# Batch 0's maximum of k, spread over the partitions by fp32 matmuls with an identity, and a new order of steps and loads

## The chip, the cores and the metric

The kernel runs on one core of a Trainium2 chip. The metric is the device time of one execution in microseconds (us). Before the change it is 240.76 us, the median of three runs (240.58 to 240.86). Engines are named as the profile names them: PE (TensorE, matmuls) and PEld (its weight loads), DVE (VectorE), ACT (ScalarE), POOL (GpSimd), SP (SyncE, which here only issues DMAs).

## What is computed

A linear attention over 8 batches, 8 heads, 576 positions and 64 channels, followed by a feed-forward block on 4608 tokens of 512 channels. All inputs and the output are fp32.

```python
q_s = exp(q - max(q, axis=-1));  q_s /= sum(q_s, axis=-1) + 1e-9
k_s = exp(k - max(k, axis=2));   k_s /= sum(k_s, axis=2) + 1e-9     # axis 2: the positions
kv  = einsum('bhsd,bhse->bhde', k_s, v)
x   = einsum('bhsd,bhde->bhse', q_s, kv)          # heads side by side: 4608 x 512
out = (((x @ w1) * (x @ w2)) @ w3) @ w_out        # 512 -> 1024 -> 1024 -> 512
```

The change is about `max(k, axis=2)` of batch 0: a maximum over positions, which lie on partitions as well as along the free dimension.

## The kernel before

**Steps and their order.** The kernel is written as named steps, such as `kmx.0.0` or `up.1.3.0.2`. Each step has an engine, the steps it needs, and the ring of PSUM or SBUF buffers from which it takes one. A long list written into the file, `ORDER`, gives the order in which the steps are emitted, and so the order of each engine's queue; `PICKS` says which engine does a step that has a choice (copies, subtractions, products). Each engine takes its own queue strictly in order and waits where a step's input isn't there. `FILL` puts in matmuls of zeros at the start. For the first `LINKED` steps of the list, steps of DVE and POOL marked as using the shared port are also chained to each other in list order.

**Folding the weights.** As `w3` and `w_out` are applied one after the other, the kernel first makes their product W3O. For each block ft of 128 rows of `w3` (0 to 7): `w3t.ft` transposes the block with eight fp16 matmuls against an identity (L439), `w3T.ft` copies it from PSUM (L322), `pf.ft.0` and `pf.ft.1` multiply it with the two halves of `w_out` (four matmuls of 512 columns each, L451), and `W3O.ft` scales it into place (L326 on ACT, L328 on DVE). The loads are `w3.3`, `w3.4` (blocks 4 and 5), `w3.1`, `w3.0`, `w3.5` (blocks 6 and 7), `w3.2` and `wo.0`, `wo.1`.

**Attention, per batch b.** A tile has the 576 positions of a head as 64 partitions times 9 along the free dimension; partitions 0 to 63 hold heads 0 to 3, partitions 64 to 127 heads 4 to 7.
- k: `kmx` takes the maximum over the 9 (a tree of four tensor_tensor for batches 0 to 3, L492 to L495), which leaves `km`, 128 x 256. `cb` takes it over the 64 partitions of each half and spreads it back: a transpose of 32x32 blocks (L499), a maximum (L502), four small instructions that swap neighbouring groups of 32 partitions (L505), one that joins them (L508), and a transpose back (L510). `ksub` subtracts it from k (two halves, L514), `kexp` is the exponential on ACT (L522), `kv` the product with v and the sums (L539, L549), `kv2` the division by the sums (L558 to L561).
- q: `qmx`, `qsub`, `qexp`, `qsm`, `qeps`, `qrc`, `qn` make the softmax over channels, in two parts (j 0 to 3 is part 0, j 4 to 8 part 1). For batches 0 and 1 `qt` transposes it on PE in groups of eight or two blocks (`qt.0.8`, `qt.0.16`, `qt.0.0`, L620) and `qT` copies it out; later batches use a DMA transpose (`qd`).
- `xm` and `xt` multiply q with kv2 (L653), `xs` and `xts` copy the result into x.

**Feed-forward, per chunk c of 512 tokens.** `up.1` and `up.0` multiply x with w2 and w1 (L767), `bs` copies the first result out of PSUM, `ab` takes the product (DVE, L782), `down` multiplies with W3O (L789, L804), `os` copies it out and `st` stores it. A ninth chunk takes the ninth j of every batch.

**Loads.** The first two loads (q of batch 0) are issued by SP, the list `LOADS` by POOL, one after the other, later ones (`LATE`) by SP. The POOL issue of load number i waits until load number i - 8 has landed: `w1.0` waits for `k.0`, `w1.1` for the load behind `k.0`, and `w2.1` for the one behind that. `k.1` waits for `wo.1`. A POOL issue also stands in POOL's queue behind the computing steps that come before it in the list.

**PSUM.** Three rings: "pab" with four buffers (`w3t`, `up`), "po" with two (`pf`, `down`), "att" with two (`kv`, `qt`, `xm` of the early batches).

**The list around the change** runs, on PE: w3t.3, w3t.4, w3t.5, pf.3.0, pf.4.0, pf.3.1, qt.0.8, pf.4.1, w3t.1, qt.0.16, pf.5.0, pf.5.1, qt.0.0, w3t.0, pf.1, pf.0.0, w3t.7, pf.0.1, w3t.2, pf.7.0, w3t.6, pf.7.1, pf.2.0, kv.0, pf.2.1, xm.0.0, pf.6, xm.0.1, and then the first `up`. (A step named without its half means both halves.)

Of the kernel before, what the change touches and what calls it, by code (L numbers as in the profile page):

```python
# [10 lines left out]
F32 = mybir.dt.float32  # L11
# [6 lines left out]
class Plan:  # L18
# [56 lines left out]
LINKED = 559  # L75

ORDER = """
q.0.1 qmx.0.1 q.0.0 qsub.0.1 qmx.0.0 qexp.0.1 w3.3 w3.4 wo.0 wo.1 w3.1 ident qsub.0.0 w3t.3 w3T.3
k.0 w3.0 w3t.4 qsm.0.1 qexp.0.0 qeps.0.1 qrc.0.1 w3T.4 w3t.5 pf.3.0 pf.4.0 qsm.0.0 qeps.0.0 pf.3.1
W3O.3 w3.5 w3.2 q.1.0 qn.0.1 qt.0.8 pf.4.1 w3t.1 qrc.0.0 w3T.5 v.0 k.1 w2.0 qn.0.0 qt.0.16 pf.5.0  # L80
w3T.1 W3O.4 qT.0.8 pf.5.1 kmx.0.0 cb.0 qt.0.0 w3t.0 W3O.5 ksub.0.1 w3T.0 pf.1.0 pf.1.1 pf.0.0 W3O.1
ksub.0.0 w3t.7 pf.0.1 w3T.7 qT.0.0 qT.0.16 kexp.0.1 W3O.0 w3t.2 pf.7.0 w3t.6 w3T.2 qmx.1.0 kexp.0.0
pf.7.1 w1.0 W3O.7 qsub.1.0 pf.2.0 w1.1 w2.1 k.2 w3T.6 kv.0 kv2.0 pf.2.1 qexp.1.0 xm.0.0 qsm.1.0
xs.0.0.1 pf.6.0 pf.6.1 xs.0.0.0 qeps.1.0 xm.0.1 xs.0.1.0 up.1.0.0.0 xs.0.1.1 up.0.0.0.0 up.1.0.1.0
w2.2 kmx.1.0 qrc.1.0 w1.2 cb.1 w2.3 w1.3 v.1 qn.1.0 bs.0.0.0 up.0.0.1.0 up.1.0.0.1 ab.0.0.0 W3O.2
qt.1.0 ksub.1.0 q.1.1 up.0.0.0.1 bs.0.1.0 up.1.0.1.1 bs.0.0.1 ab.0.1.0 qT.1.0 xt.0 ab.0.0.1 bs.0.1.1
kmx.2.0 up.0.0.1.1 up.1.0.0.2 ab.0.1.1 up.0.0.0.2 up.1.0.1.2 up.0.0.1.2 xts.0.0 xts.0.1 kexp.1.0
bs.0.0.2 ab.0.0.2 up.1.0.0.3 up.0.0.0.3 bs.0.1.2 up.1.0.1.3 ksub.1.1 cb.2 q.2 kexp.1.1 ab.0.1.2
up.0.0.1.3 v.2 W3O.6 bs.0.0.3 ab.0.0.3 kv.1 down.0.0 ksub.2.0 bs.0.1.3 kexp.2.0 kv2.1 ksub.2.1
xm.1.0 os.0.0 xs.1.0.1 xs.1.0.0 qmx.1.1 ab.0.1.3 kexp.2.1 down.0.1 qmx.2.0 qsub.1.1 up.1.1.0.0  # L90
up.0.1.0.0 up.1.1.0.1 up.0.1.0.1 qsub.2.0 vc.2.0 down.0.2 qmx.2.1 bs.1.0.0 qexp.1.1 os.0.1 vc.2.1
qexp.2.0 ab.1.0.0 qsm.1.1 bs.1.0.1 qeps.1.1 qsm.2.0 qsub.2.1 os.0.2 qrc.1.1 qn.1.1 ab.1.0.1 qeps.2.0
kv.2 up.1.1.0.2 up.0.1.0.2 up.1.1.0.3 kv2.2 qrc.2.0 up.0.1.0.3 qt.1.16 qt.1.8 down.0.3 qexp.2.1
qsm.2.1 bs.1.0.3 bs.1.0.2 qn.2.0 qeps.2.1 ab.1.0.3 ab.1.0.2 qrc.2.1 st.0.0 k.3 q.3 v.3 st.0.2 qT.1.8
qd.2.0 qn.2.1 st.0.1 qd.2.1 k.4 qT.1.16 xm.1.1 xs.1.1.0 xs.1.1.1 down.1.0 xt.1 qmx.3.1 up.1.1.1.0
qmx.3.0 kmx.3.0 up.0.1.1.0 up.1.1.1.1 os.0.3 up.0.1.1.1 bs.1.1.0 bs.1.1.1 cb.3 qsub.3.0 down.1.1
xts.1.1 xts.1.0 os.1.0 qexp.3.0 xm.2.0 ab.1.1.1 qsub.3.1 ab.1.1.0 xs.2.0.1 xs.2.0.0 up.1.1.1.2
up.0.1.1.2 qsm.3.0 xm.2.1 qexp.3.1 xs.2.1.0 xs.2.1.1 bs.1.1.2 ab.1.1.2 qsm.3.1 up.1.1.1.3 up.0.1.1.3
bs.1.1.3 ab.1.1.3 up.1.2.0.0 up.0.2.0.0 up.1.2.0.1 qeps.3.1 vc.3.0 kmx.4.0 bs.2.0.0 up.0.2.0.1
ab.2.0.0 qeps.3.0 bs.2.0.1 qrc.3.0 ksub.3.1 ksub.3.0 kexp.3.0 q.4 kexp.3.1 up.1.2.0.2 up.0.2.0.2  # L100
up.1.2.0.3 vc.3.1 os.1.1 qrc.3.1 ab.2.0.1 kmx.4.1 qmx.4.1 kv.3 down.1.2 up.0.2.0.3 qn.3.0 kv2.3 xt.2
bs.2.0.3 bs.2.0.2 qmx.4.0 ab.2.0.2 os.1.2 st.0.3 v.4 q.5 qd.3.0 qn.3.1 up.1.2.0.4 down.1.3
up.0.2.0.4 qsub.4.1 qd.3.1 qexp.4.1 ab.2.0.3 xts.2.1 xts.2.0 os.1.3 xm.3.0 xm.3.1 xt.3 bs.2.0.4
qsm.4.1 ab.2.0.4 qeps.4.1 xts.3.0 xs.3.0.1 xts.3.1 xs.3.0.0 up.1.2.0.5 bs.2.0.5 xs.3.1.1 xs.3.1.0
qsub.4.0 vc.4.0 cb.4 ksub.4.1 up.0.2.0.5 up.1.2.0.6 up.0.2.0.6 qexp.4.0 ab.2.0.5 ksub.4.0 up.1.2.0.7
up.0.2.0.7 qrc.4.1 qmx.5.1 bs.2.0.6 ab.2.0.6 vc.4.1 k.5 st.1.1 up.1.3.0.0 up.0.3.0.0 st.1.3 qsm.4.0
st.1.2 st.1.0 v.5 bs.2.0.7 qmx.5.0 ab.2.0.7 up.1.3.0.1 kexp.4.1 qeps.4.0 kexp.4.0 bs.3.0.0 qrc.4.0
kmx.5.1 down.2.0 up.0.3.0.1 kv.4 kmx.5.0 qn.4.1 os.2.0 vc.5.1 bs.3.0.1 v.6 qd.4.1 qn.4.0 qsub.5.0
cb.5 down.2.1 os.2.1 down.2.2 down.2.3 os.2.2 ab.3.0.0 kv2.4 up.1.3.0.2 qd.4.0 xm.4.0 os.2.3 xm.4.1
xt.4 ab.3.0.1 bs.3.0.2 up.0.3.0.2 xts.4.1 xts.4.0 up.1.3.0.3 up.0.3.0.3 up.1.3.0.4 qexp.5.0 ab.3.0.2  # L110
qsm.5.0 xs.4.0.0 ksub.5.0 kexp.5.0 bs.3.0.3 up.0.3.0.4 up.1.3.0.5 ab.3.0.3 xs.4.1.1 up.0.3.0.5
ksub.5.1 vc.5.0 qsub.5.1 kexp.5.1 xs.4.0.1 bs.3.0.4 qeps.5.0 ab.3.0.4 qexp.5.1 xs.4.1.0 up.1.3.0.6
# [795 lines left out]
```

## Time and profile before

| | |
|---|---|
| median of three runs | 240.76 us |
| the profiled execution, its own time | 240.74 us |
| its span, first to last instruction | 239.0 us |
| DVE busy | 180.8 us (76%) |
| ACT busy | 116.4 us (49%) |
| POOL busy | 110.2 us (46%) |
| DMA: bytes moved, mean rate | 45.66 MB, 191 GB/s |
| cb of batch 0, from its first to its last instruction's end | 22.30 to about 24.6 us |
| first `up` | 35.0 us |

The numbers come from one profiled execution; times within it count from the span's start. A line of a view names the source line (L439), the engine, the operation, the tile written and the tiles read, the shape and how many. Matmuls overlap, and their ends are modelled: the view of the chain of waits counts eight matmuls from the start of the first to the start of what follows, the timeline to the modelled end of the last. Square brackets at the end of a timeline line give the idle time of that engine just before it and what ended it.

### The profile page before, as it was taken

The page shows a single profiled execution, that of the slowest core. Times are in us where ns is not written, and L with a number is a line of the kernel's source. Part 1 is how long each engine was busy: PE and PEld are TensorE (multiplying, and loading weights), DVE is VectorE, ACT ScalarE, POOL GpSimd, SP SyncE. Part 2 cuts the span into 40 slices and gives each one's busy share as a digit, 9 for nine tenths or more (in the row PEclk, how much of TensorE's full clock was granted, in tenths as well). Part 3 has the DMA queues.
Part 4 walks back from the last instruction along what each step waited for, and adds up shares of the span by engine and source line. Part 5 has one row for each costly group of instructions (what it writes and reads, how often), then busy time and mean ns, then how long its engine had stood idle before and what let it go on. Part 6 is the DMA issues. An engine that isn't in the chain of part 4 may idle for free.

```text
span 239.0 us, 4957 instructions
## 1 busy us (share of the span) xinstructions
PE 231.4 (97%) x1987; PEld 121.4 (51%) x1987; DVE 180.8 (76%) x312; ACT 116.4 (49%) x185; POOL 110.2 (46%) x73
## 2 busy tenths in 40 slices
PE   7997999999999999999999999999999999999994
PEld 2543558867756544444444444444444444444442
DVE  2987998999899999998989989868577544443320
ACT  1625764659748848856935736452153012113211
POOL 8344178449939894989364795001910000000000
PEclk9999999999999999999999999999999999999998
DMA  6999999998999999899999302300659123030143
GB/s 206 217 293 238 321 219 295 241 392 281 393 187 323 401 220 303 298 260 347 342 390 254 91 1 44 58 0 0 134 121 198 44 58 76 0 91 0 44 132 132
DMA packets 37894, 45.66 MB, mean 191 GB/s; under 512 B 15984, under 2 KB 22384, under 8 KB 37872
## 3 DMA queue, kind: packets, MB, share of 16 engines
q1 hardware_dynamic: 30080, 34.22, 50.1%
q0 software_dynamic: 7792, 11.14, 21.2%
q8 instruction: 15, 0.25, 0.4%
q14 instruction: 7, 0.06, 0.1%
HBM read 38.80 MB, written 9.44 MB: 202 GB/s over the span
## 4 chain that ended last, share of the span: by engine, by line
PE 89%; DMA 7%; POOL 2%; issue 0%; ACT 0%; ACTq 0%; POOLq 0%
PE pab L767 53%; PE po L789 23%; DMA w<-in_moe_w_dram 7%; PE po L451 4%; PE po L804 3%; PE pkv L539 2%; PE xm L653 2%; PE w3t L439 1%; POOL w L401 1%; PE po L653 0%; PE pkv L549 0%; PE qtp L620 0%; POOL wosb L401 0%; POOL k L401 0%; PE xt L653 0%
## 5 line engine op out<-in xcount | busy, mean ns | idle before, releaser
L767 PE MATMUL pab<-x,w2sb 128*128 128x512 f16 (+1 forms) x320 | 66.0, 337 | 0.0
L767 PE MATMUL pab<-x,w1sb 128*128 128x512 f16 (+1 forms) x320 | 65.9, 337 | 0.0
L782 DVE TENSOR_TENSOR ab<-pab,bsb 128x512 f16<-128x512 f32 x72 | 48.5, 679 | 22.2 <-PE pab L767 20.1
L789 PE MATMUL po<-W3O,ab 128*128 128x512 f16 x256 | 59.4, 379 | 0.0
L322 ACT CAST bsb<-pab 128x512 f16<-128x512 f32 x52 | 30.2, 587 | 45.4 <-PE pab L767 38.4
L767 PEld LDWEIGHTS <-w1sb 128*128 128x128 f16 x352 | 34.1, 98 | 27.3
L767 PEld LDWEIGHTS <-w2sb 128*128 128x128 f16 x352 | 33.5, 98 | 27.3 <-issue 0.7
L605 POOL TENSOR_TENSOR en<-eq,qr 128x1024 f16<-128x1024 f16 (+1 forms) x13 | 26.8, 2075 | 28.1 <-issue 19.3
L789 PEld LDWEIGHTS <-ab 128*128 128x128 f16 x256 | 24.6, 98 | 29.0 <-issue 0.4
L514 POOL TENSOR_TENSOR k<-k,cb 128x1152 f32<-128x1152 f32 x13 | 34.0, 2625 | 11.0 <-DVE k L514 3.8
L322 ACT COPY osb<-po 128x512 f32<-128x512 f32 (+1 forms) x25 | 14.4, 577 | 34.9 <-PE po L789 27.6
L573 POOL TENSOR_TENSOR q<-q,qm 128x1280 f32<-128x1280 f32 (+1 forms) x13 | 27.7, 2142 | 7.5 <-DVE qm L568 4.1
L568 DVE TENSOR_REDUCE qm<-q 128x20 f32<-128x1280 f32 (+1 forms) x16 | 21.2, 1337 | 3.6 <-DMA q<-in_q_dram 3.6
L522 ACT ACTIVATE ek<-k 128x1152 f16<-128x1152 f32 x16 | 18.5, 1170 | 10.6 <-POOL k L514 9.3
L581 ACT ACTIVATE eq<-q 128x1280 f16<-128x1280 f32 (+1 forms) x16 | 18.7, 1170 | 6.6 <-POOL q L573 3.9
L586 DVE TENSOR_REDUCE qr<-eq 128x20 f32<-128x1280 f16 (+1 forms) x16 | 21.4, 1340 | 0.6 <-ACT eq L581 0.5
L322 DVE COPY osb<-po 128x512 f32<-128x512 f32 (+1 forms) x12 | 8.0, 667 | 15.5 <-PE po L789 8.3
L483 DVE TENSOR_REDUCE km<-k 128x128 f32<-128x1152 f32 x8 | 17.2, 2161 | 0.0
L322 DVE CAST bsb<-pab 128x512 f16<-128x512 f32 x20 | 13.7, 686 | 3.9 <-PE pab L767 3.6
L451 PE MATMUL po<-wosb,w3T 128*128 128x512 f16 x64 | 15.5, 379 | 0.5 <-DMA wosb<-in_moe_w_out_dram 0.5
L326 ACT ACTIVATE x<-xm 128x512 f16<-128x512 f32 x21 | 11.9, 603 | 3.2 <-PE xm L653 3.2
L349 PE MATMUL po<-zero 128*128 128x512 f16 x31 | 9.2, 457 | 1.6 <-DVE zero L344 1.6
(70 smaller groups left out, 193.2 us busy)
## 6 DMA issues: line engine op xcount, KB each, us to landing
out_dram<-osb SPq DMA_DIRECT2D x66, 128.0 KB, 2.5
q<-in_q_dram SPq DMA_DIRECT2D x6, 1152.0 KB, 8.0
v<-in_v_dram SPq DMA_DIRECT2D x6, 1152.0 KB, 8.9
k<-in_k_dram SPq DMA_DIRECT2D x5, 1152.0 KB, 7.2
k<-in_k_dram POOLq DMA_DIRECT2D x3, 1152.0 KB, 14.5
v<-in_v_dram POOLq DMA_DIRECT2D x2, 576.0 KB, 14.8
w<-in_moe_w_dram POOLq DMA_DIRECT2D x4, 256.0 KB, 14.4
w<-in_moe_w_dram POOLq DMA_DIRECT2D x2, 512.0 KB, 12.9
```

What stands on the lines that cost most here:

```text
L322: return [(nc.scalar.copy if eng == "ACT" else engine[eng].tensor_copy)(out=out, in_=in_)]
L451: nc.tensor.matmul(st["pf", ft], lhsT=st["w3T", ft][:, gt, :], rhs=wosb[:, gt, :], start=(gt == 0), stop=(gt == N_FT - 1))
L514: return [engine[eng].tensor_tensor(out=kb[:, two(hp), :, :], in0=kb[:, two(hp), :, :], in1=st["cb", b][:, two(hp), None, :].broadcast_to( ...
L522: nc.scalar.activation(out=st["ek", b][:, hp, :, :].rearrange("p j (i d) -> p i j d", i=2), in_=kb[:, two(hp), :, :], func=AF.Exp)
L568: dve.tensor_reduce(out=st["qm", b][:, :, j], in_=qb[:, :, j, :], axis=AX.X, op=ALU.max)
L573: return [engine[eng].tensor_tensor(out=qb[:, :, j, :], in0=qb[:, :, j, :], in1=st["qm", b][:, :, j, None].broadcast_to([P, HH, n, D]), op ...
L581: nc.scalar.activation(out=st["eq", b, p], in_=qb[:, :, j, :], func=AF.Exp)
L586: dve.tensor_reduce(out=st["qr", b][:, :, slice(*PARTS[p])], in_=st["eq", b, p], axis=AX.X, op=ALU.add)
L605: return [engine[eng].tensor_tensor(out=st["en", b][:, j, :, :].rearrange("p j h d -> p h j d"), in0=st["eq", b, p], in1=st["qr", b][:, :, ...
L767: nc.tensor.matmul(st["p", one, c, sub, u][:, a * (t1 - t0):(a + 1) * (t1 - t0)], lhsT=w[:, ct, fb * P:(fb + 1) * P], rhs=x()[:, ct, t0:t1 ...
L782: dve.tensor_tensor(out=st["ab", c][:, nf * u:nf * u + nf, t0:t1], in0=cut(st["p", 0, c, sub, u]), in1=cut(st["bsb", c, sub, u]), op=ALU.mult)
L789: nc.tensor.matmul(st["po", c, tb], lhsT=st["ab", c][:, ft, tb * P:(tb + 1) * P], rhs=W3O[:, ft, :], start=(ft == 0), stop=(ft == N_FT - 1))
```

## The change

For batch 0 (`PEK = [0]`) the step `cb` is replaced by three:
- `kT`: km, as two halves of 128 columns, is transposed by two fp32 matmuls against an fp32 identity into PSUM.
- `kr`: DVE takes the maximum over each group of 64 of the transposed columns, 128 x 256 to 128 x 4.
- `kB`: four fp32 matmuls with the identity as the moving operand. Each takes one column of kr, repeated 64 times, as the weights, so that the maximum appears on 64 partitions. The result stays in PSUM, and `ksub`, now always on DVE for batch 0, reads it there.

`kT` and `kB` take a buffer of the ring "pab". A new step `ident32` copies the identity to fp32 on ACT. The other batches keep `cb`. The rest of the new code (`CBX`, `KVE`, `kc`) is for settings that are off.

`ORDER`, `PICKS` and `LATE` are written anew over the whole program, `LINKED` goes from 559 to 580, and in `LOADS` w3.5 and w3.0 change places.

```diff
-LINKED = 559
+LINKED = 580
...
 LOADS = [
-    ("w3", 3), ("w3", 4), ("wo", 0), ("wo", 1), ("w3", 1), ("k", 0), ("w3", 0), ("w3", 5),
+    ("w3", 3), ("w3", 4), ("wo", 0), ("wo", 1), ("w3", 1), ("k", 0), ("w3", 5), ("w3", 0),
...
+    plan.add(("ident32",), "ACT", 0.28, lambda: nc.scalar.copy(out=ident32, in_=ident16), needs=[("ident",)],
+             lead=200.0)
...
+        def kT():
+            st["kT", b] = kbank("kT")
+            for n in range(NHP):
+                nc.tensor.transpose(st["kT", b][:, n, :], st["km", b].rearrange("p h d -> p (h d)")[
+                    :, n * P:(n + 1) * P], ident32)
...
+        def kr():
+            st["kr", b] = work.tile([P, NHP, G], F32, tag="kr", name="kr")
+            dve.tensor_reduce(out=st["kr", b], in_=st["kT", b].rearrange("p n (g r) -> p n g r", g=G),
+                              axis=AX.X, op=ALU.max)
...
+        def kB():
+            st["kB", b] = kbank("kB")
+            for n in range(NHP):
+                for gg in range(G):
+                    nc.tensor.matmul(st["kB", b][gg * HALF:(gg + 1) * HALF, n, :],
+                                     lhsT=st["kr", b][:, n, gg:gg + 1].broadcast_to([P, HALF]),
+                                     rhs=ident32, start=True, stop=True)
+            if not b:
+                st["cb", b] = st["kB", b].rearrange("p n (i d) -> p (n i) d", d=D)
...
-        A(("cb", b), "DVE", 2.25, cb, kms)
+        if b in PEK:
+            A(("kT", b), "PE", 0.45, kT, kms + [("ident32",)], takes=kring)
+            A(("kr", b), "DVE", 0.45, kr, [("kT", b)], gives=[("kT", b)])
+            A(("kB", b), "PE", 0.45, kB, [("kr", b)], takes=kring)
```

The new list on PE around this place: w3t.3, w3t.4, w3t.5, pf.3.0, pf.4.0, qt.0.8, pf.3.1, pf.4.1, w3t.1, qt.0.16, pf.5.0, qt.0.0, pf.5.1, pf.1, w3t.7, kT, kB, w3t.0, pf.7, pf.0.0, w3t.2, w3t.6, pf.0.1, kv.0, pf.2, xm.0.0, pf.6, xm.0.1, and then the first `up`.

Other moves near the start: the fp16 identity is made on POOL ahead of the first weight load instead of behind the fifth; `qsub.0.0` goes from DVE to POOL, ahead of the issue of the load w3.2; `qn.0.0` on POOL stands ahead of the issue of w2.0 instead of behind it; `w3T.3` and `w3T.1` go from ACT to DVE, `w3T.4` and `w3T.5` from DVE to ACT, `W3O.3`, `W3O.4` and `W3O.5` from ACT to DVE. On ACT the order between w3t.7 and kv.0 is w3T.7, W3O.1, qT.0.0, qT.0.16, w3T.0, kexp.0.0, W3O.7, kexp.0.1; on DVE it is kmx.0, W3O.5, kr, ksub.0.0, ksub.0.1, qmx.1.0, qsub.1.0, w3T.2, w3T.6, kv2.0. Over the rest of the program the matmuls are the same ones in another order, and DVE gets 6 more `bs` and 3 more `xs` and loses 6 `os`.

More of the change, by code (lines that the diff above doesn't have):

```diff
@@ L83 @@
[L83 to L88, printed above, removed]
```

210 lines of the change are left out of this document (131 added, 79 removed), and 96 rows, old and new, of the table PICKS.

## The prediction

> **What bounds the kernel now.** I read the page first: one engine carries nearly all of the span.
>
> ```profile
> span 239.0 us, 4957 instructions
> ...
> PE 231.4 (97%) x1987; PEld 121.4 (51%) x1987; DVE 180.8 (76%) x312; ACT 116.4 (49%) x185; POOL 110.2 (46%) x73
> ```
>
> TensorE is busy in 231.4 of 239.0 us, so the first question is where the other 7.6 us lie. The table of windows answers it (window, its length, then busy time and count for PE, PEld, DVE, ACT and POOL, clock, DMA share, GB/s):
>
> ```profile
> 7.70:20.20 12.50, 11.91 (x88) 6.65 (x88) 9.80 (x12) 6.39 (x9) 6.11 (x7) 1.00 1.08 259
> 20.20:21.96 1.76, 0.00 (x0) 0.00 (x1) 1.66 (x4) 0.17 (x1) 0.18 (x1) 1.00 1.11 207
> 21.96:30.10 8.14, 8.14 (x60) 4.80 (x60) 7.89 (x16) 5.87 (x8) 1.55 (x3) 1.00 1.11 307
> 30.10:35.00 4.90, 4.90 (x137) 2.58 (x137) 4.62 (x10) 2.87 (x5) 3.80 (x6) 1.00 1.41 207
> 35.00:60.00 25.00, 25.00 (x320) 19.61 (x316) 23.03 (x47) 16.70 (x25) 17.51 (x10) 1.00 1.13 301
> 60.00:100.00 40.00, 40.00 (x414) 22.92 (x413) 38.24 (x67) 29.54 (x53) 32.22 (x16) 1.00 1.01 299
> 100.00:200.00 100.00, 100.00 (x788) 46.00 (x786) 79.52 (x138) 45.06 (x71) 43.10 (x21) 1.00 0.57 151
> ...
> 236.00:239.00 3.00, 0.00 (x0) 0.00 (x0) 0.00 (x0) 0.10 (x1) 0.00 (x0) 0.79 0.29 96
> ```
>
> From 21.96 on TensorE has no gap until the last matmuls: 8.14 of 8.14, 4.90 of 4.90, 25.00 of 25.00 and so on, at a granted clock of 1.00. Before that lies one hole, 20.20 to 21.96, with 0.00 busy. So an edit behind 21.96 pays only in the amount of TensorE work, and the time ends when all the matmuls that were not yet done at 21.96 have run. The chain of waits says what ended the hole (start, length, what):
>
> ```profile
> 5.62 16.30 DMA w<-in_moe_w_dram
> ...
> 21.96 0.71 PE w3t L439 x8
> 22.68 2.59 PE po L451 x12
> 25.27 0.49 PE w3t L439 x8
> ...
> 28.46 1.73 PE po L451 x8
> ...
> 34.73 0.34 PE xm L653 x8
> ```
>
> The chain goes from a load of `moe_w3` (16.30 us) into the transposes of w3t.0 at 21.96, and stays on TensorE. Behind w3t.0 stand twelve matmuls, pf.1 (eight) and half of pf.0. Nothing in them needs the late load except the half of pf.0: pf.1 needs w3.1, which has been here for long. They wait only because TensorE takes its queue in order.
>
> The k chain of batch 0, which the change shortens, reads in the timeline:
>
> ```profile
> 19.39 1.23 DVE L492 TENSOR_TENSOR kmx<-k 128x1024 f32<-128x1024 f32 x1 [1.97 <-DMA k<-in_k_dram]
> ...
> 21.84 0.43 DVE L495 TENSOR_TENSOR km<-kmx,k 128x256 f32<-128x256 f32 x1
> ...
> 22.30 0.45 DVE L499 STREAM_TRANSPOSE kmq<-km 128x256 f32<-128x256 f32 x1
> ...
> 22.78 0.42 DVE L502 TENSOR_REDUCE mx<-kmq 128x8 f32<-128x256 f32 x1
> ...
> 24.61 2.63 DVE L514 TENSOR_TENSOR k<-k,cb 128x1152 f32<-128x1152 f32 x2
> ...
> 28.56 1.18 ACT L522 ACTIVATE ek<-k 128x1152 f16<-128x1152 f32 x1
> ...
> 30.12 0.78 PE L539 MATMUL pkv<-v,ek 64*64 64x64 f16 x72
> ```
>
> The maximum km is ready at 22.27 (21.84 + 0.43), cb takes from 22.30 to 24.61, that is 2.31 us, the two ksub 2.63 to 27.24, kexp ends at 29.74 (28.56 + 1.18), and kv.0 starts at 30.12. TensorE had work up to 30.10. So the chain that is made shorter had about 0.4 us of slack before kv.0 and bounds nothing by itself; what counts is where the matmuls go.
>
> **The change part by part.** The loads first, because they set when TensorE may go on:
>
> ```profile
> 1.25 1.42 POOL L401 DMA_DIRECT2D w<-in_moe_w_dram  x2 [0.81 <-POOLq L892]
> ...
> 4.27 0.25 POOL masks.py:197 MEMSET ident<- 128x128 f16 x1
> ...
> 4.60 0.29 POOL masks.py:199 TENSOR_SCALAR_AFFINE_SELECT ident<-ident 128x128 f16<-128x128 f16 x1
> ...
> 7.69 0.71 PE L439 MATMUL w3t<-ident,w 128*128 128x128 f16 x8 [0.29 <-DMA w<-in_moe_w_dram]
> ...
> 10.17 1.19 PE L439 MATMUL w3t<-ident,w 128*128 128x128 f16 x16
> ...
> 15.07 1.02 PE L451 MATMUL po<-wosb,w3T 128*128 128x512 f16 x4 [0.47 <-DMA wosb<-in_moe_w_out_dram]
> ...
> 15.32 0.75 POOL L401 DMA_DIRECT2D k<-in_k_dram  x1 [1.70 <-DMA wosb<-in_moe_w_out_dram]
> ...
> 22.21 0.74 POOL L401 DMA_DIRECT2D w1sb<-in_moe_w_dram  x1 [1.82 <-DMA w<-in_moe_w_dram]
> ...
> 24.03 0.74 POOL L401 DMA_DIRECT2D w2sb<-in_moe_w_dram  x1 [1.08 <-DMA w<-in_moe_w_dram]
> ```
>
> Loads come in one after the other: w3.3 (one block of rows of w3) is seen at 7.69, w3.4 (two blocks) at 10.17, so two blocks take 2.48 us and one 1.24. w3.0 is seen by TensorE at 21.96; the POOL issue that the code lets wait for it starts at 22.21, 0.25 later (wo.1: 15.07 and 15.32, again 0.25). The issue that waits for w3.5 starts at 24.03, so w3.5 was there at 23.78.
>
> *Loads listed anew.* w3.5 now stands ahead of w3.0. Both together end where they ended, at 23.78, and the last of them is now one block, so w3.5 should be there at 23.78 - 1.24 = 22.54. Were w3.0's lateness not handed on, it would be k.0's arrival plus 2.48, 19.39 + 2.48 = 21.87. These are the two ends; I take 22.5, since the late end already contains what delayed w3.0. The identity is now made ahead of w3.3 instead of behind the first five loads: the first issue moves from 1.25 by at most 4.60 + 0.29 - 4.27 = 0.62. If the engines were still busy with q then, nothing is lost; if not, all of it. I take 0.3, so w3.5 at 22.8.
>
> *pf.1 ahead of the load.* The new list runs pf.5, both halves of pf.1, and then w3t.7, which needs w3.5. TensorE comes to this point at about 21.5 to 22.1: the hole began at 20.20, pf.1 adds 1.73 (the row of 28.46, eight such matmuls), the 0.3 of the loads may be added and qt.0.8 leaves this stretch (below). So it waits for w3.5 until 22.8. Compared with before, TensorE goes on 22.8 - 21.96 = 0.84 later, and with 1.73 less to do: -0.89.
>
> *The new steps.* kT (two fp32 transposes), kr and kB (four fp32 matmuls, 64 columns of weights each) stand directly behind each other, and TensorE has nothing between kT and kB: it waits for kr. What is queued behind kB is w3t.0, pf.7, pf.0 and everything after. kr is a maximum over 128x256, as the L502 row is (0.42 at 22.78, from SBUF; here from PSUM); with a handover of 0.04 on each side, like 22.27 to 22.30, TensorE stands for 0.50. W3O.5 is put between km and kr on DVE, but it falls into the wait for w3t.7. No row has an fp32 matmul. Bounds: a 128-column fp16 matmul costs 0.49 / 8 = 0.061 (row of 25.27), one of 512 columns 1.73 / 8 = 0.216. kT and kB together then cost 6 x 0.061 = 0.37 to 6 x 0.216 = 1.30, and a little below the lower end if two 64-wide halves run at once, as the eight xm matmuls do (0.34 for 8 x 256 columns, against 0.86 at the 512-column rate). I take the upper end: 128 fp32 columns hold more bytes than any row's 128, and I know of no row in which that came free. So 0.50 + 1.30 = 1.80; the bounds are 0.87 and, with six unhidden weight loads of about 0.15, 2.7.
>
> [...]
>
> *What hangs on ACT.*
>
> ```profile
> 22.76 1.01 ACT L322 COPY w3T<-w3t 128x1024 f16<-128x1024 f16 x1 [2.39 <-DVE kmq L499]
> ...
> 24.44 0.60 ACT L326 ACTIVATE W3O<-po 128x512 f16<-128x512 f32 x1 [0.67 <-PE po L451]
> ...
> 26.75 0.38 ACT L322 COPY qT<-qtp 128x256 f16<-128x256 f16 x1
> ```
>
> Between w3t.7 and kv.0 the new list gives ACT w3T.7, W3O.1, two qT, w3T.0, then kexp, W3O.7, kexp. w3t.7 ends at 22.8 + 0.71 = 23.5. Then 1.01 + 0.60 + 1.01 + 0.38 + 1.01 (a qT of eight blocks is copied as w3T is) gives 27.5, kexp 28.7, W3O.7 29.3, kexp 30.5. TensorE, after kB at 25.3, has w3t.0, pf.7, pf.0, w3t.2 and w3t.6: 3 x 0.49 + 2 x 1.73 = 4.9, and is at kv.0 at 30.2. So kv.0 waits 0.3. ksub starts at 25.3, later than the 24.61 of before, although the new block is shorter than cb (1.80 against 2.31): the chain now stands behind w3t.7. On DVE kr waits for kT, and behind it are the two ksub, qmx.1.0, qsub.1.0 and the copies w3T.2 and w3T.6; the first of these that TensorE needs is w3T.2, at pf.2 behind kv.0, and that is in time. ksub runs on DVE from 25.3 to 28.0 and is not what kexp waits for.
>
> *Steps that cost nothing.* qsub.0.0 moves from DVE to POOL and qn.0.1 runs earlier:
>
> ```profile
> 9.31 1.23 DVE L573 TENSOR_TENSOR q<-q,qm 128x1024 f32<-128x1024 f32 x1
> ...
> 14.17 1.48 DVE L605 TENSOR_TENSOR en<-eq,qr 128x1280 f16<-128x1280 f16 x1
> ...
> 15.94 0.61 PE L620 MATMUL qtp<-ident,en 128*128 128x128 f16 x8
> ...
> 17.34 1.92 POOL L605 TENSOR_TENSOR en<-eq,qr 128x1024 f16<-128x1024 f16 x1
> ```
>
> qsub takes 1.23 on DVE; on POOL I price it like the POOL row of the same size, 1.92, so 9.3 to 11.3. w3.2's issue waits behind it, with six loads still under way, so the queue does not run dry. DVE does qsm meanwhile, waits little for qsub's end before qeps, goes on with qrc, and qn.0.1 (1.48) ends at about 13.5 in place of 15.65. qt.0.8 (0.61) then fits before wo.1 (15.07). That shortens TensorE's way to the wait for w3.5, which swallows it; without that wait it is worth up to 0.45. Making the fp32 identity is one small ACT copy while ACT has nothing. The later batches keep the same matmuls; their list is new, and before shows no hole there that could be closed, so I set them at nothing, and a loss is a rival.
>
> *Sum.* +0.84 - 1.73 + 1.80 + 0.3 = +1.2. The profiled execution took 240.74 (239.0 span, 1.74 around it), 0.02 from the median of 240.76. Forecast: 241.9.
>
> **The rivals.**
>
> *Faster:* pf.1 fills the hole and nothing takes its place. It decides where the delay of w3t.7 plus the new block falls below 1.73. With w3.5 at 21.9, no shift, and the new block at its lower bound of 0.87: -0.1 - 1.7 + 0.9 = -0.9, so 239.8. For it speaks that pf.1 was ready; against it the price of fp32, and that w3.0 was late.
>
> *No difference:* w3.5 is in time but fp32 costs its upper bound. -0.1 - 1.73 + 1.80 + 0.3 = +0.3, so 241.0.
>
> *A new hole later:* DVE is busy in 23.03 of 25.00 us from 35 to 60 and 38.24 of 40.00 from 60 to 100. In a rearranged list a product or an eviction that comes late stops TensorE, as PSUM buffers are few. Three stops of the length of a PSUM copy of 512 columns (0.60, the row of 24.44) add 1.8 to the forecast: 243.7. For it speaks DVE's load; against it that before has as much and no hole, and that DVE gives and takes about the same work.
>
> *The change doesn't do what it says:* the k maximum is spread no earlier. This is part of the forecast (25.3 against 24.61), and it is false if w3t.7 is not waited for.
>
> **How the numbers follow.** The forecast has 0.58, the later hole 0.10, no difference 0.15, faster 0.17. A measurement of this kernel tells apart about 0.2%, 0.48 us. The shift of the loads (0 to 0.62), the arrival (21.87 to 22.54) and the block (0.87 to 2.7) open the forecast to about 240.6 to 243.2; with part of the rivals on each side 8 in 10 gives 240.3 to 243.5. Faster 0.17, within 0.2% 0.15, slower 0.68.
>
> **What would show it.** In the new profile: pf.1 runs before 22.1 and TensorE then waits for a load of w at w3t.7 (right) or not (then "no difference" or "faster"); the fp32 rows give kT and kB; between them a wait of TensorE on kr of 0.5; kv.0 waits for ek; the first up starts at 36.3 in place of 35.07 (34.73 + 0.34); the windows from there on are full again. It is wrong if holes appear behind the first up, or if the loads come in at another pace.

## The result and the profile after

The changed kernel takes 241.71 us, the median of 20 runs (240.21 to 243.47); the kernel before, run beside it on the same chip, 240.63 us (20 runs, 240.38 to 241.37). The ratio is 1.0046, with a 95% interval from 1.0024 to 1.0069. The forecast was 241.9. Ratios follow the means of the runs and not the medians, and leave out one run (244.71, of fill_less below) that lies more than 1.5% above the fastest of its kernel.

The median hides what the 20 times look like. They lie in three groups, all counted here: 5 from 240.21 to 240.43, 9 from 241.59 to 241.92, and 6 from 242.84 to 243.47. The kernel before has one group here. The mean granted clock separates the last group from the others: 0.991 to 0.993 there, 0.997 to 1.0 in the others. The profiled execution took 240.43, so it belongs to the first group, which is faster than the profiled execution of before (240.74). Every profile of this kernel that was taken belongs to that group; no execution of the two upper groups was caught by the profiler. So what follows from the trace holds for the first group, and what happens in the upper two had to be found by making it happen.

The page of after:

```profile
span 238.7 us, 4968 instructions
...
PE 233.0 (98%) x1997; PEld 121.8 (51%) x1997; DVE 180.7 (76%) x308; ACT 112.9 (47%) x181; POOL 113.1 (47%) x75
```

TensorE is busy 1.6 us longer in a span that is 0.3 us shorter: holes were filled. The new matmuls kT and kB are 1.10 us of it (0.44 and 0.66 in the timeline below). The table of windows of after, over the same stretches as that of before (window, its length, busy time and count for PE, PEld, DVE, ACT and POOL, clock, DMA share, GB/s):

```profile
7.70:20.20 12.50, 12.36 (x92) 6.91 (x91) 10.43 (x15) 4.25 (x4) 7.82 (x8) 1.00 1.08 258
20.20:21.96 1.76, 1.54 (x8) 0.57 (x7) 1.69 (x3) 0.00 (x0) 0.30 (x1) 1.00 1.13 215
21.96:30.10 8.14, 7.62 (x150) 4.98 (x152) 7.31 (x10) 7.05 (x10) 2.40 (x4) 1.00 1.11 305
30.10:35.00 4.90, 4.90 (x65) 2.20 (x58) 4.59 (x11) 2.11 (x5) 2.80 (x4) 1.00 1.41 207
35.00:60.00 25.00, 25.00 (x321) 19.88 (x319) 23.39 (x47) 15.41 (x23) 17.87 (x10) 1.00 1.17 328
60.00:100.00 40.00, 40.00 (x410) 22.41 (x409) 37.57 (x70) 29.08 (x50) 33.83 (x17) 1.00 1.01 309
100.00:200.00 100.00, 100.00 (x788) 45.99 (x787) 74.97 (x126) 49.21 (x83) 42.29 (x20) 1.00 0.53 140
```

The hole of before is closed: 1.54 of 1.76 are busy. A smaller one has come, 0.52 between 21.96 and 30.10. From 30.10 on TensorE is full, as it was before. The waits of TensorE in after (total, how often, longest) name what is left:

```profile
PE po L354 <- DVE zero L349: 1.6, 1, 1.6
PE kB L548 <- DVE kr L541: 0.5, 1, 0.5
PE w3t L446 <- DMA w<-in_moe_w_dram: 0.2, 1, 0.2
```

The first row is the start of the program, where before has it too. The second is the new wait for kr, as forecast. The third is the point on which the forecast turned: TensorE was expected at w3t.7 between 21.5 and 22.1 and was to wait there until 22.8, so for 0.7 to 1.3; the wait is 0.2. The timeline of after around it (start, length; in brackets the idle time ahead and what ended it):

```profile
1.44 1.42 POOL L406 DMA_DIRECT2D w<-in_moe_w_dram  x2
...
7.88 0.71 PE L446 MATMUL w3t<-ident,w 128*128 128x128 f16 x8
...
9.60 1.91 POOL L634 TENSOR_TENSOR q<-q,qm 128x1024 f32<-128x1024 f32 x1 [3.08 <-DVE qm L629]
...
12.15 1.49 DVE L666 TENSOR_TENSOR en<-eq,qr 128x1280 f16<-128x1280 f16 x1
...
21.88 0.71 PE L446 MATMUL w3t<-ident,w 128*128 128x128 f16 x8 [0.22 <-DMA w<-in_moe_w_dram]
...
22.49 0.44 PE L536 MATMUL kT<-ident,km 128*128 128x128 f32 x2
...
22.96 0.42 DVE L541 TENSOR_REDUCE kr<-kT 128x4 f32<-128x256 f32 x1
...
23.44 0.66 PE L548 MATMUL kB<-ident,kr 128*64 128x128 f32 x8 [0.52 <-DVE kr L541]
...
24.03 0.71 PE L446 MATMUL w3t<-ident,w 128*128 128x128 f16 x8
...
24.14 2.62 DVE L567 TENSOR_TENSOR k<-k,kB 128x1152 f32<-128x1152 f32 x2 [0.76 <-PE kB L548]
...
27.68 1.20 ACT L575 ACTIVATE ek<-k 128x1152 f16<-128x1152 f32 x1
...
28.19 1.03 PE L458 MATMUL po<-wosb,w3T 128*128 128x512 f16 x4
...
29.14 0.78 PE L592 MATMUL pkv<-v,ek 64*64 64x64 f16 x72
...
34.74 1.05 PE L846 MATMUL pab<-x,w2sb 128*128 128x256 f16 x8
```

The rows from 21.88 on are the new heart of the kernel: w3t.7, kT, kr, kB, w3t.0, the two ksub and, at the end, kv.0 and the first `up`. The first `up` starts at 34.74, before it was 35.00: 0.26 earlier, and the time of the execution is 0.31 shorter.

### The profile page after: what moved, and what is told of

Same layout as the page of the kernel before. It is cut to its first block, busy times and chain, and to the rows that moved or that the text cites. A ratio compares the mean times of both kernels' runs of the same rounds, so it can differ in the third digit from the quotient of the medians.

```text
span 238.7 us, 4968 instructions
## 1 busy us (share of the span) xinstructions
PE 233.0 (98%) x1997; PEld 121.8 (51%) x1997; DVE 180.7 (76%) x308; ACT 112.9 (47%) x181; POOL 113.1 (47%) x75
## 4 chain that ended last, share of the span: by engine, by line
PE 89%; DMA 6%; DVE 2%; POOL 1%; issue 0%; ACT 0%; POOLq 0%; DVEq 0%
PE pab L846 53%; PE po L868 23%; DMA k<-in_k_dram 6%; PE po L458 3%; PE po L883 3%; PE pkv L592 2%; PE xm L714 2%; POOL w L406 1%; PE w3t L446 1%; DVE kmx L499 1%; POOL wosb L406 0%; PE po L714 0%; PE pkv L602 0%; PE qtp L681 0%; DVE kmx L500 0%; PE kB L548 0%
## 5 line engine op out<-in xcount | busy, mean ns | idle before, releaser
L327 ACT CAST bsb<-pab 128x512 f16<-128x512 f32 x46 | 26.7, 587 | 37.2 <-PE pab L846 35.8
L567 POOL TENSOR_TENSOR k<-k,cb 128x1152 f32<-128x1152 f32 x12 | 31.5, 2632 | 18.0 <-DVE cb L525 9.7
L327 ACT COPY osb<-po 128x512 f32<-128x512 f32 (+1 forms) x31 | 17.4, 571 | 43.3 <-PE po L868 38.1
L634 POOL TENSOR_TENSOR q<-q,qm 128x1024 f32<-128x1024 f32 (+1 forms) x14 | 29.7, 2126 | 17.1 <-DVE qm L629 12.0
L666 POOL TENSOR_TENSOR en<-eq,qr 128x1024 f16<-128x1024 f16 (+1 forms) x14 | 29.2, 2095 | 13.8 <-DVE qr L659 13.7
L327 DVE CAST bsb<-pab 128x512 f16<-128x512 f32 x26 | 17.9, 688 | 9.6 <-PE pab L846 9.3
L331 ACT ACTIVATE x<-xm 128x512 f16<-128x512 f32 x18 | 10.3, 598 | 5.9 <-PE xm L714 5.9
L354 PE MATMUL po<-zero 128*128 128x512 f16 x31 | 9.8, 480 | 1.6 <-DVE zero L349 1.6
L327 DVE COPY osb<-po 128x512 f32<-128x512 f32 x6 | 4.1, 688 | 7.6 <-PE po L868 4.8
```

Of the source, the lines that this page charges most:

```text
L327: return [(nc.scalar.copy if eng == "ACT" else engine[eng].tensor_copy)(out=out, in_=in_)]
L567: return [engine[eng].tensor_tensor(out=kb[:, two(hp), :, :], in0=kb[:, two(hp), :, :], in1=st["cb", b][:, two(hp), None, :].broadcast_to( ...
L634: return [engine[eng].tensor_tensor(out=qb[:, :, j, :], in0=qb[:, :, j, :], in1=st["qm", b][:, :, j, None].broadcast_to([P, HH, n, D]), op ...
L666: return [engine[eng].tensor_tensor(out=st["en", b][:, j, :, :].rearrange("p j h d -> p h j d"), in0=st["eq", b, p], in1=st["qr", b][:, :, ...
```

## The experiments

**The theory** going in: the first group is an execution in which w3.5 has landed when TensorE comes to w3t.7. In the middle group w3.5 lands later, and TensorE waits there, as it stood 1.76 us at w3t.0 in before with pf.1 listed behind it. **The rivals:** the new fp32 steps themselves vary, or the clock alone makes the groups (TensorE stands still at kr, and the clock falls afterwards), whatever the load does. A third account in the expectations is a wait behind the first `up`. By the runs, the clocks of the last group (0.991 to 0.993, spans of 241.1 to 241.7) are worth (1 - 0.993) x 241.1 / 0.5 = 3.4 to (1 - 0.991) x 241.7 / 0.5 = 4.4 us at half clock; half clock itself is in the trace of before, 0.50 from 237.80 to 238.90, behind its last matmul.

The experiments ran in several jobs. A job is a set of runs made together on one chip, each beside the kernel before; those reported from here on ran on three different chips, so what differs from job to job may be the chip.

### The kernel unchanged, run again

No edit. The aim was a profile of an upper group.

> The changed kernel as it is, once more, for a profile of another execution. Its 20 times lie in three groups (about 240.3, 241.7 and 243.1), and the profile at hand is of the first. Landing theory: in the slower groups load w3.5 comes late, w3t.7 waits 1.2 to 1.8 us for a load of w, and all behind it is late by as much; the clock stays near 1.00. Clock theory: the slower groups have a stretch of about 3.4 us at half the granted clock, which costs 1.4 to 1.7 us each time. Later-hole theory: up to the first up the profile is the same as the one at hand, and a TensorE wait appears behind it. If the time is near 240.3 again, this look tells nothing.

> As for again_1: landing theory, w3t.7 waits 1.2 to 1.8 us for a load; clock theory, a stretch of 3.4 us at half clock; later-hole theory, a TensorE wait behind the first up. Near 240.3 it tells nothing.

> The changed kernel as it is, timed on the same chip as the three runs beside it. Both theories: three groups near 240.3, 241.7 and 243.1, the shares as they fall on this chip.

The two single runs took 240.27 and 240.25, both of the first group, and say nothing on the others. The third, again_3, has 12 runs, in another job: ten from 240.15 to 240.52, one of 241.86 and one of 242.91 at a clock of 0.993; median 240.41 against 240.65 for the kernel before, ratio 1.0003 (0.9984 to 1.0022). So the groups stay where they were and their shares change: 15 of 20 executions were in the upper two at first, 2 of 12 now. The loss that was measured first is a property of the kernel and of something outside it that differs from job to job.

### The old way of spreading the maximum, in the new list

```diff
-    PEK = [0]
+    PEK = []
-... w3t.7 W3O.5 kT.0 kr.0 kB.0 ksub.0.0
+... w3t.7 W3O.5 cb.0 ksub.0.0
-LINKED = 580
+LINKED = 578
```

> The new list and loads, but cb in place of kT, kr and kB. My account: w3t.7 is followed at once by w3t.0, which waits for w3.0 (there at about 23.5 us); cb ends near 24.9, the second kexp near 30.0, and kv.0 starts about 0.9 us later than the 29.14 of the changed kernel, while two pieces of TensorE work (0.44 and 0.66 us) are gone. So about 240.43 + 0.9 = 241.3 in the fast group. Rival, that the block itself costs more than it gives: 239.5 to 240.0. If the three groups of times come from waiting for kr with TensorE idle (clock theory), they are gone here; if from the landing of w3.5, they stay.

240.90 (12 runs, 240.60 to 242.37), ratio 1.0021 (1.0005 to 1.0037). The profiled execution took 240.66, and kv.0 isn't 0.9 later, as I had expected; it starts a little earlier than in after. The timeline of old_block:

```profile
21.59 0.71 PE L446 MATMUL w3t<-ident,w 128*128 128x128 f16 x8 [0.24 <-DMA w<-in_moe_w_dram]
...
23.58 0.71 PE L446 MATMUL w3t<-ident,w 128*128 128x128 f16 x8 [1.28 <-DMA w<-in_moe_w_dram]
...
24.95 2.63 DVE L567 TENSOR_TENSOR k<-k,cb 128x1152 f32<-128x1152 f32 x2
...
27.89 1.16 ACT L575 ACTIVATE ek<-k 128x1152 f16<-128x1152 f32 x1
...
29.03 0.77 PE L592 MATMUL pkv<-v,ek 64*64 64x64 f16 x72
...
34.98 1.05 PE L846 MATMUL pab<-x,w2sb 128*128 128x256 f16 x8
```

Without kT and kB TensorE comes to w3t.0 earlier and waits there 1.28, for w3.0. So in after kT, the wait for kr and kB stand in a time in which TensorE would have waited for the next load anyway: their 1.54 us replace a wait of 1.28. The two executions aren't in step: w3t.7 starts at 21.59 here and at 21.88 in after. Counted from it, ksub starts 3.36 later here and 2.26 later in after, 1.10 apart; the second kexp ends at 29.05 (27.89 + 1.16) and 28.88 (27.68 + 1.20), which is 7.46 and 7.00 later, so only 0.46 of the 1.10 comes through ACT's queue; the first `up` starts 13.39 and 12.86 later, 0.53 apart. By the profiled executions the new way of spreading the maximum is worth 0.23 us (240.66 and 240.43). By the lowest groups it is nearer 0.5: seven runs from 240.60 to 241.03, their median 240.75, against 240.27 and 240.25 for the changed kernel in the same job. The groups are there without the fp32 steps as well: beside the seven there are four from 241.39 to 241.87, and one of 242.37 at a clock of 0.992. That speaks against the rival by which the fp32 steps vary, and against the wait for kr as the cause, since there is none here.

### The new block ahead of the load that TensorE waits for

kT and kB need k.0 and not w3.5, so w3t.7 can stand behind them.

```diff
-... kmx.0.0 w3t.7 W3O.5 kT.0 kr.0 kB.0 ksub.0.0 ...
+... kmx.0.0 W3O.5 kT.0 kr.0 kB.0 w3t.7 ksub.0.0 ...
```

The second ksub is also listed ahead of pf.7.

> The changed kernel with w3t.7 moved behind kB (and the second ksub listed ahead of pf.7). TensorE then waits for km (about 22.45 us) in place of w3.5, and w3t.7 runs at 24.05, when w3.5 has been there for long. Landing theory: the slow groups go, every time lies near 240.4 + 0.5 = 240.9, as 0.5 us of TensorE work moves behind the wait for km. Clock theory: the groups stay as they are, median 241.7 to 242.2, or get worse, as TensorE now idles 0.8 us before kT and 0.5 before kB. Later-hole theory: the groups stay too, with no clock difference.

242.29 (6 runs, 242.20 to 242.39), ratio 1.0067 (1.0053 to 1.0081). There is one group: six times within 0.2 us. That is what the theory asks for, since w3t.7 comes so late now that w3.5 has been there for long (no row of the waits names a load). Six runs are few, though: old_block, in the same job, had 5 of 12 in its upper groups, and with such a share six runs without a slower one aren't rare. But the level, for which 240.9 was expected, is missed by 1.4. The waits of TensorE in kt_first (line numbers differ by kernel):

```profile
PE po L391 <- ACT w3T L260: 1.4, 2, 0.7
PE kT L469 <- DVE km L435: 0.9, 1, 0.9
PE kB L481 <- DVE kr L474: 0.5, 1, 0.5
```

Moving w3t.7 back moves its copy on ACT back, and pf.7 and pf.0 wait for copies: 1.4 in two waits. Another 0.9 goes by before km is ready. The order in the changed kernel uses this time, for w3t.7. The run agrees with the theory, without proving it, and shows no way out.

### The blocks 0 and 7 exchanged, with their loads

w3t.0 takes the place of w3t.7 and the other way round, and so do w3T, pf and W3O of the two blocks. w3.0, which is one block of rows, is loaded ahead of w3.5, which is two: at the place where TensorE could wait, it now needs 256 KB where it needed 512.

```diff
-    ... ("w3", 1), ("k", 0), ("w3", 5), ("w3", 0),
+    ... ("w3", 1), ("k", 0), ("w3", 0), ("w3", 5),
-... pf.1.1 kmx.0.0 w3t.7 W3O.5 kT.0 kr.0 kB.0 ...
+... pf.1.1 kmx.0.0 w3t.0 W3O.5 kT.0 kr.0 kB.0 ...
```

> The changed kernel with blocks 0 and 7 of w3 exchanged: w3.0 is loaded ahead of w3.5 again, and w3t.0, w3T.0, pf.0 and W3O.0 take the places of w3t.7, w3T.7, pf.7 and W3O.7, and the reverse. TensorE then comes out of pf.1 to a block whose load is one piece shorter. Landing theory: w3.0 is there about 1.2 us earlier than w3.5 was, w3t.0 starts without a wait, even an execution in which the load is disturbed by 1 us loses nothing, and all times lie in one group near 240.2. Clock theory: the wait for kr is still there, and so are the three groups, median 241.7.

> swap07 once more, beside the changed kernel on one chip. Landing theory: one group, 240.2 to 240.7, whatever the share of slow executions of the changed kernel here. If only the chip decided whether there are slow executions, both have the same share.

240.40 (11 runs, 240.22 to 240.63), ratio to the kernel before 0.9987 (0.9975 to 0.9999); again in the job of again_3, 240.43 (11 runs, 240.21 to 240.60), ratio 0.9991 (0.9982 to 0.9999). One group in both. The timeline of swap07:

```profile
21.26 0.66 PE L379 MATMUL w3t<-ident,w 128*128 128x128 f16 x8
...
22.27 0.44 PE L469 MATMUL kT<-ident,km 128*128 128x128 f32 x2 [0.36 <-DVE km L435]
...
23.23 0.66 PE L481 MATMUL kB<-ident,kr 128*64 128x128 f32 x8 [0.52 <-DVE kr L474]
...
34.64 1.05 PE L779 MATMUL pab<-x,w2sb 128*128 128x256 f16 x8
```

The transposes start at once, with no bracket; km and kr are waited for, 0.36 and 0.52. So TensorE stands still longer at the new block than in after (0.88 against 0.22 + 0.52 = 0.74), and no execution out of 22 lost its clock (0.998 to 1.0). The rival by which the wait for kr alone makes the groups falls. What was taken away is the load's lateness, and the groups went with it. The new list behind the first `up` is that of the changed kernel, so a wait there isn't the cause either. In the same two jobs the kernels that keep the loads and the order of after have 9 of 36 runs in the upper groups (3 in fill_more, 4 in fill_less, 2 in again_3), swap07 has 0 of 22; were the share the same, this would happen about once in a hundred times. Beside again_3 the median is the same (240.43 and 240.41); what is gained is the two upper groups.

### What makes the load late: more and fewer zero matmuls at the start

The idea behind this pair: in the profile of after a packet of the queue that fetches instructions (16 KB, 0.95 us) starts at 21.24, just when w3.5 comes in. Were it tied to a place in TensorE's stream of instructions, four zero matmuls more or fewer at the start would move it against the landing, and change the shares of the groups. (The expectations put the packet about 0.24 us later than it is when counted from the span's start.)

```diff
-    "begin": 17, "w3t.4": 8, "pf.3.0": 6,
+    "begin": 21, "w3t.4": 8, "pf.3.0": 6,     (fill_more; 13 in fill_less)
```

> The changed kernel with 21 matmuls of zeros at the start in place of 17. In the trace of before, a 16 KB instruction fetch takes one DMA engine for 0.9 us from 20.1, while w3.0 is under way, and w3.0 is seen 1.3 us late; in the fast traces of the changed kernel it comes at 21.2 to 21.5, when that engine is done with w3.5. If it is TensorE's fetch and comes at a fixed place in its instructions, four matmuls more at the start bring it forward by up to 0.9 us, into w3.5. Landing theory: nearly every execution is then in the slower groups, 241.6 to 243. Clock theory: more activity at the start, so no worse than the changed kernel, or better. If the fetch isn't TensorE's, nothing changes: three groups, median 241.7.

> The changed kernel with 13 matmuls of zeros at the start in place of 17. Landing theory with the fetch at a fixed place in TensorE's instructions: it comes up to 0.9 us later, behind w3.5, and nearly every execution is in the fast group, 240.2 to 240.5. Clock theory: less activity at the start, more executions slow, median 241.7 or above. If the fetch isn't TensorE's: three groups as before.

fill_more: 240.49 (12 runs: nine up to 241.07, one of 242.06, two of 243.12 and 243.16 at a clock of 0.991), ratio 1.0016 (0.9990 to 1.0042). fill_less: 240.49 (12 runs: eight up to 240.51, and 241.65, 242.86, 243.18, 244.71), ratio 1.0013 (0.9987 to 1.0038). The pair has no measurable effect against the kernel before; the unchanged kernel wasn't run in this job. The packet did not move: it starts at 21.25 and 21.05, and in the four profiles of the changed kernel between 20.93 and 21.25. I had expected fill_more nearly all in the upper groups, and it is not. What falls is that the zero matmuls move the packet in this kernel. Whether the packet makes the load late was not tested, as it stayed.

The traces speak for the packet. In the traces each of these loads ends with sixteen reports, and the time of each is kept. In the profile of before the packet starts at 19.84; fifteen reports of w3.0 are there by 20.39, and the last comes at 21.92, which is what ended the hole. In before_fill_less, the next kernel below, it starts at 20.63, when all sixteen of w3.0 are in (the last at 20.51); there the next load, w3.5, has its last report 0.76 behind the fifteenth. In the four profiles of the changed kernel the last report of w3.5 comes at most 0.18 behind the fifteenth, and that of w3.0, the load behind it, 0.53 to 0.89. So the one load that TensorE stood waiting for in before was late by a single report, with the packet under way. That a packet which starts a little earlier hits w3.5 in the same way in the upper groups is likely, and not shown.

### The kernel before with four zero matmuls fewer

```diff
-    "begin": 17, "w3t.4": 8, "pf.3.0": 6,
+    "begin": 13, "w3t.4": 8, "pf.3.0": 6,
```

> The kernel before with 13 matmuls of zeros at the start in place of 17. If the fetch moves behind w3.0, the wait of 1.76 us at w3t.0 goes. My account: TensorE is then at kv.0 by about 28.4 and waits there for the second kexp (29.74), so of 1.76 us no more than about 0.1 to 0.4 is gained: 240.3 to 240.6. Rival, that the wait at w3t.0 was the whole loss: 239.0. If the fetch stays where it is, 240.6.

240.44 (10 runs, 240.24 to 241.27), ratio 0.9987 (0.9969 to 1.0005), as expected. Its trace shows one thing more. The timeline of before_fill_less:

```profile
20.56 0.71 PE L439 MATMUL w3t<-ident,w 128*128 128x128 f16 x8 [0.23 <-DMA w<-in_moe_w_dram]
...
28.61 1.04 PE L451 MATMUL po<-wosb,w3T 128*128 128x512 f16 x4 [0.53 <-DVE w3T L322]
...
32.13 0.60 PE L653 MATMUL xm<-qT,kv 64*64 64x256 f16 x8 [0.28 <-DVE kv L561]
...
34.85 1.05 PE L767 MATMUL pab<-x,w2sb 128*128 128x256 f16 x8
```

w3.0 is there at 20.56, in the profile of before it was seen at 21.96. The loads and their order are the same in both, only the zeros at the start differ; the landing differs by 1.4 us. And of the hole's 1.76 us, 1.5 went without much gain: the first `up` starts at 34.85, where it was 35.00, as the waits of 0.53 and 0.28 behind it take most of what was saved (these count from the modelled ends of the matmuls before them, and are longer from start to start). So before was not held by that hole as firmly as it looked; when the load comes early, the copies and the k chain come last instead. A loss like that of the upper groups is rare in it, but not unknown: of its 35 runs in this job the two highest were 241.96 and 242.75.

### The load made late, and the wait filled with zeros

old_loads is the changed kernel with w3.0 loaded ahead of w3.5, as before: w3.5 lands late in each execution. old_loads_fill adds seven zero matmuls ahead of w3t.7, in a buffer of the ring "pab".

```diff
-    ... ("w3", 1), ("k", 0), ("w3", 5), ("w3", 0),
+    ... ("w3", 1), ("k", 0), ("w3", 0), ("w3", 5),
...                                             (old_loads_fill only)
-    "begin": 17, "w3t.4": 8, "pf.3.0": 6,
+    "begin": 17, "w3t.4": 8, "pf.3.0": 6, "w3t.7": 7,
-        idle = p_o()
+        idle = p_ab() if n == 7 else p_o()
```

> The changed kernel with w3.0 loaded ahead of w3.5 as before, the list otherwise the same: w3.5 is late on purpose, by one block (1.24 us), in every execution, and what comes behind it in the queue is not. Landing theory: w3t.7 waits 1.4 to 1.7 us for a load, and the times are 240.3 + 1.4 = 241.7 in nearly every execution at a clock of 1.00: the second group made at will. If the third group (clock 0.991 to 0.993) is a half-clock stretch set off by this wait and the one for kr together, a part of the executions lies near 243.1. Against the landing theory: times near 240.3, or three groups in the old shares.

> old_loads with seven matmuls of zeros (1.5 us) ahead of w3t.7, in the wait for w3.5. They add no work to the path as long as the wait is 1.5 us or more. If the lower clock of the third group comes from the idle stretch, no execution is near 243 and none has a clock under 0.996; times near 241.7 to 241.9. If the lower clock has another cause, the share near 243 is that of old_loads.

old_loads: 244.91 (5 runs: 243.54 and four from 244.79 to 245.01), ratio 1.0167 (1.0148 to 1.0185), over 3 us above what I had expected. The timeline of old_loads:

```profile
23.79 0.70 PE L446 MATMUL w3t<-ident,w 128*128 128x128 f16 x8 [1.91 <-DMA w<-in_moe_w_dram]
...
25.23 1.12 PE L548 MATMUL kB<-ident,kr 128*64 128x128 f32 x8 [0.52 <-DVE kr L541]
...
37.85 1.05 PE L846 MATMUL pab<-x,w2sb 128*128 128x256 f16 x8
```

w3t.7 starts 1.91 later than in after, after a wait of 1.91, and kB's records take 1.12 where they took 0.66. The windows of old_loads show why (the column behind POOL is the granted clock):

```profile
21.96:25.10 3.14, 0.92 (x10) 0.69 (x10) 1.60 (x4) 0.52 (x1) 0.74 (x1) 0.96 1.09 285
25.10:28.50 3.40, 3.27 (x20) 2.14 (x21) 2.18 (x3) 3.28 (x6) 0.00 (x0) 0.53 1.17 263
28.50:30.10 1.60, 1.60 (x10) 0.69 (x8) 1.60 (x2) 1.43 (x2) 0.00 (x0) 1.00 1.05 435
```

Over 3.14 us TensorE had ten matmuls to do, all transposes, 0.92 us busy. Then the clock is at half: in windows of 0.5 us from 25.10 to 28.10 it is 0.50 in each. By the table the stretch is (1 - 0.96) x 3.14 / 0.5 + (1 - 0.53) x 3.40 / 0.5 = 3.4 us long. The first `up` starts 37.85 - 34.74 = 3.11 later, the difference in time (243.54 - 240.43 = 3.11). Of it 1.91 is the later w3t.7; the other 1.20 is the stretch at half clock, which counts the same work from w3t.7 to the first `up` as 14.06 us (37.85 - 23.79) instead of 12.86 (34.74 - 21.88). Four of the five runs have twice as much lost clock (0.984 to 0.985, against 0.993 in the profiled one), so by these means two such stretches; none of those four was profiled.

old_loads_fill: 242.40 (5 runs, 242.14 to 242.53; clock 0.999 to 1.0), ratio 1.0074 (1.0061 to 1.0087). The timeline of old_loads_fill:

```profile
21.22 1.67 PE L354 MATMUL pab<-zero 128*128 128x512 f16 x7
...
23.59 0.71 PE L446 MATMUL w3t<-ident,w 128*128 128x128 f16 x8 [0.69 <-DMA w<-in_moe_w_dram]
...
25.04 0.66 PE L548 MATMUL kB<-ident,kr 128*64 128x128 f32 x8 [0.52 <-DVE kr L541]
...
36.45 1.05 PE L846 MATMUL pab<-x,w2sb 128*128 128x256 f16 x8
```

and its windows:

```profile
25.10:28.50 3.40, 3.40 (x27) 1.80 (x28) 2.76 (x3) 3.40 (x6) 0.00 (x0) 1.00 1.18 268
```

The load lands as late as in old_loads (23.59, 23.79), but the clock stays at 1.00, and kB takes 0.66 again. The first `up` is 1.71 later than in after, and so is the time (242.14 - 240.43 = 1.71), and w3t.7 is too (23.59 - 21.88 = 1.71): in this execution a late w3.5 costs what it is late, no more and no less, while the clock holds. Seven matmuls of zeros are worth 2.5 us against old_loads (medians 242.40 and 244.91). In neither kernel is w3.5 late by the 1.24 that was expected but by 1.91 and 1.71: its last report comes 0.48 and 0.76 behind the fifteenth, which is a part of the difference.

The wait of 1.91, the ten transposes in the 3.14 us around it and the wait of 0.52 for kr come together in old_loads; which of them brings the clock down, no run here separates.

## Why the prediction came out as it did

**The median.** Forecast 241.9, measured 241.71, slower by 0.45% (forecast 0.5%), inside the range. That the median fell there was in part luck: 15 of these 20 runs were in the upper groups, and with the share of again_3 (2 of 12) it would have been near 240.4. At the median the stated reason is also the likely one: w3.5 late at w3t.7. It is inferred, not seen: old_loads_fill shows that such lateness costs its own length at full clock, and the middle group lies 1.3 us above the first (241.7, 240.4), which by that measure is a w3t.7 at 21.88 + 1.3 = 23.2, where I forecast 22.8; with the 1.54 that the new steps took (below) the sum is then 23.2 - 21.96 - 1.73 + 1.54 = +1.05. So the load has 0.4 more than I had put, the new steps and ACT 0.56 less, and that the total is so near is luck too. The last group lies another 1.4 higher, about the 1.20 of the half-clock stretch in old_loads, and has its clock (0.991 to 0.993, and 0.993). swap07 takes the lateness away, and both groups go.

**The step that failed,** in the profiled execution: *loads listed anew*, w3.5 at 22.8. There w3t.7 starts at 21.88, the early end of my bounds (21.87). The fault is not the choice between the ends. I took a landing to be one number of the kernel, and it is one of the execution: w3.0 at 21.96 and 20.56 in two traces of the same loads. My bounds of 21.87 to 22.54 for w3.5 were worked out from a single one, and the late end has in it a delay of that execution: of the sixteen reports of w3.5 in the trace of before, the fifteenth comes at 22.86 and the last at 23.75. Of the 0.3 that I gave to the identity, 0.19 came (first issue 1.44 against 1.25, w3t.3 7.88 against 7.69).

**The other steps,** on the profiled execution:
- *pf.1 ahead of the load*: right. TensorE reached the wait at 21.66 (21.88 - 0.22), and pf.1's 1.73 lies ahead of it.
- *The new steps*: forecast 1.80, measured 1.54 (22.49 to 24.03). kT took 0.43 until the wait began, as forecast, the wait 0.52 (0.50), kB 0.59 (0.86): it was mis-sized by 0.27.
- *ksub* at 25.3: 24.14, since w3t.7 was not waited for. By the prediction's own condition the rival "doesn't do what it says" is then false.
- *What hangs on ACT*, a wait of 0.3 at kv.0: none. The second kexp ended at 28.88, and kv.0 started at 29.14, when pf.0 was through. This term hung on the late w3t.7 too.
- *Steps that cost nothing*: right. qsub took 1.91 on POOL (1.92), qn.0.1 ended at 13.64 (about 13.5).
- *A new hole later*: fell; the windows from 30.10 to 200 are full.

**The sum** in that execution: 21.88 - 21.96 = -0.08, -1.73, +1.54: -0.27, against -0.26 at the first `up` and -0.31 in the time. With w3.5 in time the outcome is the rival *no difference*, which I had put at 241.0 because of the two terms that were too large (kB by 0.27, ACT by 0.3). The rival *faster* had 239.8, and no run of any kernel here reached it (the lowest is 240.15): where the hole went, the wait for w3.0 behind it (old_block) or the copies (before_fill_less) took a part of its place.

**What the prediction lacked** is the clock. It added waits as if a wait cost only its length. A wait of 1.9 at this place, followed by transposes and the wait for kr, costs another 1.2 in the profiled execution of old_loads and, by their clock, about twice that in its four other runs; the six slowest runs of the 20 show a loss of the first size in their clock.

**What stays open:** what makes w3.5 land late in some executions, and in 15 of 20 in one job and 2 of 12 in another. The packet that fetches instructions fits the profile of before and is the likeliest cause, but no run here moved it in the changed kernel. No profile of an execution of the upper groups of the unchanged kernel exists.

**The best version** is swap07, 0.13% and 0.09% below the kernel before (0.9987 and 0.9991, both intervals end at 0.9999), 0.2 to 0.3 us. That is less than the 0.2% that I took as the limit of a measurement, with both intervals just short of 1; what is clear is that it keeps its time in all 22 runs.

## What to carry to other kernels

A landing read from one trace is a sample: if an engine that runs in order will stand at a load, ask what a landing 1.4 us later costs (w3.0 at 21.96 and 20.56, with the same loads), and put the smallest load or the most slack there. When a change of a full engine gives several groups of times, look at the groups and their clocks before the median. A wait of TensorE that is followed by transposes and another wait can cost the clock as well (1.20 us in old_loads, on top of the 1.91 that the load was later), and zero matmuls in the wait are cheaper than that (old_loads_fill: clock 1.00, and 2.5 us less by the medians).

## What the runs showed of the hardware

The answer about the tile kB of after (count, shortest, median and longest ns, first and last start):

```profile
L548 PE MATMUL kB<-ident,kr x8: 272/273/323, 23.4 to 23.8; 128*64 128x128 f32 x8
```

- The four fp32 matmuls of kB, 64 columns of weights each, show as eight records, which start two at a time, the pairs 0.16, 0.11 and 0.11 us apart. They cost 0.59 us on the path, less than four times a 512-column fp16 matmul (0.86, with 1.73 for eight in before): 0.38 from the first start to the last, and 0.21 until the next matmul starts. Which two run together the records don't tell. One record takes 0.27 us from start to end, and the two fp32 transposes of kT together 0.44, so the larger part of kT's price is the time of one record from start to end.
- The same loads in the same order landed 1.4 us apart in two executions (w3.0 at 21.96 and 20.56). In the late one a single one of sixteen reports was late (20.39 for the fifteenth, 21.92 for the last), with a packet of the queue that fetches instructions under way from 19.84 to 20.74.
- A wait of 1.91 us, with only ten transposes in the 3.14 us around it, was followed by 3.4 us at half clock (old_loads); seven zero matmuls of 512 columns, with a wait of 0.69 us left, kept the clock at 1.00 (old_loads_fill).
